# Float64 weights decoded with one VectorE step fewer, without low parts by DMA, and with rows negated on GpSimd

## The chip, the cores and the metric

One core of one Trainium2 chip runs the whole kernel. The number that counts is the device time of an execution in microseconds, the median of three runs. The engines named below are TensorE (PE in the rows), VectorE (DVE), ScalarE (ACT), GpSimd (POOL) and SyncE (SP), which only starts DMAs here.

## The reference

Causal attention over 2 batches, 12 heads, 448 positions and head size 64 gives 896 tokens of width 768. Two feed-forward layers with 2048 hidden units follow, with two different gates:

```python
x = attn_out.transpose(0, 2, 1, 3).reshape(896, 768)
h = x @ w_in;   g = h * cos(h);                                x = g @ w_out
h = x @ w_in2;  g = h if h >= 1 else 0 if h <= -1 else (h + 1)**2 / 4
return (g @ w_out2).astype(float32)
```

Queries, keys and values are float32. The weights are float64 (a product of float32 numbers with a numpy scalar), and the answer has to be close to that of float64 arithmetic.

## The kernel before

**Arithmetic.** TensorE multiplies in a rounded float32 format. So each operand is split in a high part `hi` (a copy in that format) and a low part `lo` (the value minus `hi`), and each product is three matmuls: hi*hi, hi*lo, lo*hi.

**Decoding.** A float64 weight lies in SBUF as two 32-bit words, `low` and `high`. From them a float32 is put together: sign and exponent from `high`, 20 bits of mantissa from `high`, 3 from `low`. ScalarE takes `Abs` of `high` read as float32 (line 236, rows of `w_out` 726). VectorE clamps that to the range of exponents (240, 584), masks and shifts it left by 3 (242, 585), ORs in the top 3 bits of `low` (247, 590) and then the sign and the top exponent bit of `high` (250, 593).

**Input stage of a layer.** `w_in` comes in 16 units of 768 x 128 numbers (units 0 to 15 for the first layer, 16 to 31 for the second). `load_unit` brings one into one of two `raw` buffers, the decoded unit lies in one of two `f` buffers, and ScalarE copies `whi` (258). For `wlo` there are three ways. Units 0 and 1 use GpSimd (267). Units 3 to 15 (`UNIT_LO_BY_DMA`) use ScalarE for -f (262) and then a DMA that adds `f` to it (264). The others use VectorE (267). TensorE multiplies the units two by two (line 632); a pair is 72 matmuls. A gate follows for each unit: ScalarE and VectorE in turn, lines 686 to 705.

**Output stage of a layer.** `w_out` comes in 16 blocks of rows (n = 0 to 15, even blocks first; the last six use the `raw` buffers too). They are decoded into `ws` and one of two halves is negated by ScalarE (`rows_minus`, 573). The output product is done in Strassen's way with seven products over four slices, 28 steps t = 0 to 27. Each step needs four splits, `shi`, `slo` from `ws` and `s`, `s` from the gates `gs` (lines 758 to 768), and is 18 matmuls (line 800). Sums of two `ws` or two `gs` parts are accumulating DMAs from GpSimd's queue (576).

**What sets the order.** Attention runs in an order given by tables (`PLACES`, `SHIFTS`, `DECODE`, `FILL`); units 0, 1 and 2 are begun there. Behind it everything is planned by the class `Plan`: each operation has an engine, a cost in us and a list of operations that it needs; a delay (`LAG`) stands for the way from one engine to the next, above all for DMAs. `Plan` works back from TensorE's order to the latest start of each operation, and then issues on each engine, of what is ready, the most urgent. The result is a fixed order for each engine: an engine that waits for one instruction does nothing behind it. In the plan's names A, K, M, H, O are the steps of a unit (abs, first and second half of the decoding, `whi`, `wlo`), a, k, m, g those of a row block.

Of the kernel before, what the change touches and what calls it, by code (L numbers as in the profile page):

```python
# [15 lines left out]
U32 = mybir.dt.uint32  # L16
AF = mybir.ActivationFunctionType
# [15 lines left out]
EXP_MIN = _float_of(897 << 20)  # L33
EXP_MAX = _float_of((1150 << 20) | 0xFFFFF)
# [46 lines left out]
UNIT_LO_BY_DMA = set(range(3, 16))  # L81
# [3 lines left out]
class Plan:  # L85


    LAG = {"PE": 0.1, "ACT": 0.15, "DVE": 0.1, "SP": 4.6, "POOL": 5.0}
# [8 lines left out]
    def add(self, name, engine, us, make, after=(), at=-9.0):  # L97
        after = [a for a in after if a in self.ops]
        op = dict(engine=engine, us=us, make=make, after=[(a, self.LAG[self.ops[a]["engine"]]) for a in after], at=at)
        if engine == "PE":  # L100
            if self.last_pe:
                op["after"].append((self.last_pe, 0.0))
            self.last_pe = name
        assert name not in self.ops
        self.ops[name] = op

    def run(self):
# [17 lines left out]
        while any(waiting.values()):  # L125
            best = None
            for e, names in waiting.items():
                can = []
                for n in names:
                    if all("end" in ops[a] for a, _ in ops[n]["after"]):  # L130
                        r = max([ops[a]["end"] + lag for a, lag in ops[n]["after"]] + [ops[n]["at"]])
# [12 lines left out]
            self.log.append((start, e, n, ops[n]["late"]))  # L144
            ops[n]["make"]()
# [17 lines left out]
def attention_then_two_ffn(  # L163
# [60 lines left out]

    def decode_unit(u):
# [4 lines left out]
        words = raw.bitcast(U32).rearrange("p (m two) -> p m two", two=2)  # L230
        low, high = words[:, :m, 0], words[:, :m, 1]
        full = f_p.tile([P, UW], F32, tag="f", name=f"f{u}")
        fl = full[:, :m]
        bits = full.bitcast(U32)[:, :m]

        nc.scalar.activation(  # L236
            out=fl, in_=raw.bitcast(F32).rearrange("p (m two) -> p m two", two=2)[:, :m, 1], func=AF.Abs
        )
# [3 lines left out]
        nc.vector.tensor_scalar(  # L242
            out=bits, in0=bits, scalar1=0x07FFFFFF, scalar2=3,
            op0=ALU.bitwise_and, op1=ALU.logical_shift_left,
        )
        yield
        nc.vector.scalar_tensor_tensor(  # L247
            out=bits, in0=low, scalar=29, in1=bits, op0=ALU.logical_shift_right, op1=ALU.bitwise_or,
        )
        nc.vector.scalar_tensor_tensor(  # L250
            out=bits, in0=high, scalar=0xC0000000, in1=bits, op0=ALU.bitwise_and, op1=ALU.bitwise_or,
        )
# [328 lines left out]
    def decode_bits(bits, low, high, part):  # L581
        if part == 0:
            fl = bits.bitcast(F32)
            nc.vector.tensor_scalar(out=fl, in0=fl, scalar1=EXP_MAX, scalar2=EXP_MIN, op0=ALU.min, op1=ALU.max)
            nc.vector.tensor_scalar(
                out=bits, in0=bits, scalar1=0x07FFFFFF, scalar2=3,
                op0=ALU.bitwise_and, op1=ALU.logical_shift_left,
            )
        else:
            nc.vector.scalar_tensor_tensor(  # L590
                out=bits, in0=low, scalar=29, in1=bits, op0=ALU.logical_shift_right, op1=ALU.bitwise_or,
            )
            nc.vector.scalar_tensor_tensor(  # L593
                out=bits, in0=high, scalar=0xC0000000, in1=bits, op0=ALU.bitwise_and, op1=ALU.bitwise_or,
            )

# [11 lines left out]
    def ffn(k):  # L608
# [8 lines left out]
        def add(name, engine, us, make, after=(), at=-9.0):  # L617
            plan.add(f"{k}{name}", engine, us, make, [a[1:] if a[0] == "@" else f"{k}{a}" for a in after], at)
# [100 lines left out]
        def rows_parts(n):  # L719
            j, i, q = spot(ORDER[n])  # L720
            words = raw_rows[n].bitcast(U32).rearrange("p (h m two) -> p h m two", two=2, h=2)
            return ws[j].bitcast(U32)[:, q : q + 2, i], words[:, :, :, 0], words[:, :, :, 1]

        def rows_abs(n):
            bits, _, high = rows_parts(n)
            nc.scalar.activation(out=bits.bitcast(F32), in_=high.bitcast(F32), func=AF.Abs)  # L726

        def rows_bits(n, which):
            decode_bits(*rows_parts(n), which)

        def rows_minus(n):
            j, i, q = spot(ORDER[n])
            minus(ws[j][:, q + 1, i])
# [156 lines left out]
        for f in range(0, KF, 2):  # L890
# [14 lines left out]
            for i in (f, f + 1):  # L905
# [7 lines left out]
                else:  # L913
                    add(f"G{i}", "ACT", 2.85, partial(start_gate, i), need)
# [12 lines left out]
        for n in range(KF):  # L927
# [27 lines left out]
        def add_split(t):  # L955
# [130 lines left out]
```

## Time and profile before

| | us |
|---|---|
| three runs | 547.92, 547.98, 548.77 |
| median | 547.98 |
| the profiled execution | 548.55 |
| its span in the trace | 546.8 |
| mean granted TensorE clock | 0.987 |

The span runs from the first to the last instruction in the trace; 1.75 us of the profiled execution lie around it. In time order the stages are: attention to about 84 us, the first layer's input products to 211, its output products to 325, the second layer's input products to 441, its output products to the end.

### The profile page before, as it was taken

What the parts mean: (1) busy time and instruction counts of PE and PEld (TensorE: products, weight loads), DVE (VectorE), ACT (ScalarE), POOL (GpSimd) and SP (SyncE); (2) the same over time, 40 slices, a digit from 0 to 9 for tenths busy, and PEclk for the clock granted to TensorE, in tenths of its full rate; (3) what the DMA queues carried; (4) which work ended last, traced back from release to release, by engine and by line L of the source; (5) the groups of instructions that cost most, each with busy time, mean ns of one, the idle gap of its engine ahead of it and who ended that gap; (6) DMA issues with size and microseconds to landing.
All of it is one profiled execution on the core that took longest, in us unless ns stands there. A gap on an engine that the chain in (4) does not pass through costs nothing.

```text
span 546.8 us, 7835 instructions
## 1 busy us (share of the span) xinstructions
PE 523.4 (96%) x2865; PEld 454.6 (83%) x2865; DVE 449.4 (82%) x637; ACT 374.1 (68%) x618; POOL 106.4 (19%) x159
## 2 busy tenths in 40 slices
PE   8999999989999799994999999999999999999997
PEld 3676668778988789993899999898898999999996
DVE  6878788798898788981999889899999878996661
ACT  5999875786887587861656554978797897645430
POOL 2667672012122011241000000000101014300000
PEclk9999999989999899998899999999999999999999
DMA  8731136989999584799203047396768459950111
GB/s 302 254 120 41 39 109 226 244 216 229 277 261 282 136 208 121 155 225 238 50 2 115 1 125 261 128 236 179 237 202 236 120 154 205 205 116 17 52 50 51
DMA packets 45574, 87.80 MB, mean 161 GB/s; under 512 B 2784, under 2 KB 32096, under 8 KB 45536
## 3 DMA queue, kind: packets, MB, share of 16 engines
q1 hardware_dynamic: 36464, 61.40, 33.6%
q0 software_dynamic: 8784, 25.56, 25.8%
q8 instruction: 22, 0.36, 0.3%
q10 hardware_dynamic: 288, 0.34, 0.2%
q14 instruction: 16, 0.13, 0.1%
HBM read 58.98 MB, written 2.75 MB: 113 GB/s over the span
## 4 chain that ended last, share of the span: by engine, by line
PE 75%; DMA 11%; DVE 5%; issue 4%; ACT 4%; POOL 1%; DVEq 0%; POOLq 0%; ACTq 0%
PE m L800 35%; PE m L632 28%; DMA wlo<-f 7%; DMA raw<-in_moe_w_in 3%; PE o L437 3%; PE tx L412 2%; PE sa L323 2%; ACT p L373 1%; PE sb L323 1%; PE tw L412 1%; ACT f L236 1%; PE tz L412 1%; PE warm L516 1%; PE sc L308 1%; DVE f L250 1%
## 5 line engine op out<-in xcount | busy, mean ns | idle before, releaser
L632 PE MATMUL m<-x,whi 128*128 128x512 f32 (+2 forms) x728 | 207.3, 366 | 0.0
L800 PE MATMUL m<-s,shi 128*128 128x448 f32 x648 | 186.4, 369 | 7.4 <-ACT shi L758 7.4
L632 PEld LDWEIGHTS m<-x,whi 128*128 128x128 f32 x728 | 136.2, 190 | 14.4
L632 PE MATMUL m<-x,wlo 128*128 128x512 f32 (+2 forms) x364 | 133.7, 367 | 7.9 <-DMA wlo<-f 7.9
L800 PEld LDWEIGHTS m<-s,shi 128*128 128x128 f32 x648 | 122.5, 189 | 18.8 <-ACT shi L758 7.8
L800 PE MATMUL m<-s,slo 128*128 128x448 f32 x324 | 119.5, 369 | 0.0
L632 PEld LDWEIGHTS m<-x,wlo 128*128 128x128 f32 x364 | 69.4, 191 | 16.3 <-DMA wlo<-f 9.2
L800 PEld LDWEIGHTS m<-s,slo 128*128 128x128 f32 x324 | 61.2, 189 | 5.9 <-DVE slo L766 0.5
L766 DVE TENSOR_TENSOR slo<-ws,shi 128x768 fp32r<-128x768 f32 x56 | 53.0, 951 | 11.6 <-ACT shi L758 11.6
L576 POOL DMA_DIRECT2D ws<-ws x24 | 21.7, 903 | 189.2 <-ACT ws L573 136.7
L236 ACT ACTIVATE f<-raw 128x768 f32<-128x768 f32 x32 | 29.1, 912 | 31.7 <-DMA raw<-in_moe_w_in 17.4
L758 ACT CAST shi<-ws 128x768 fp32r<-128x768 f32 x56 | 46.0, 825 | 2.7 <-PE m L800 2.7
L758 ACT CAST s<-gs 128x896 fp32r<-128x896 f32 x24 | 22.6, 942 | 30.6 <-PE m L800 30.6
L760 ACT ACTIVATE s<-gs 128x896 fp32r<-128x896 f32 x30 | 28.5, 950 | 19.3 <-PE m L800 12.9
L576 POOL DMA_DIRECT2D gs<-gs x24 | 22.3, 930 | 89.3 <-DVE s L768 30.5
L768 DVE SCALAR_TENSOR_TENSOR s<-gs,s 128x896 fp32r<-128x896 f32 x30 | 32.6, 1085 | 5.7 <-ACT s L760 5.7
L258 ACT CAST whi<-f 128x768 fp32r<-128x768 f32 x32 | 26.5, 828 | 12.8 <-DVE f L250 11.5
L766 DVE TENSOR_TENSOR s<-gs,s 128x896 fp32r<-128x896 f32 x24 | 26.1, 1087 | 9.5 <-ACT s L758 9.5
L726 ACT ACTIVATE ws<-rows 128x768 f32<-128x768 f32 x32 | 28.9, 909 | 6.8 <-DMA rows<-in_moe_w_out 6.8
L250 DVE SCALAR_TENSOR_TENSOR f<-raw,f 128x768 uint32<-128x768 uint32 x32 | 31.1, 971 | 1.1
L593 DVE SCALAR_TENSOR_TENSOR ws<-rows,ws 128x768 uint32<-128x768 uint32 x32 | 30.7, 958 | 1.1
L247 DVE SCALAR_TENSOR_TENSOR f<-raw,f 128x768 uint32<-128x768 uint32 x32 | 30.7, 960 | 0.0
(103 smaller groups left out, 770.6 us busy)
## 6 DMA issues: line engine op xcount, KB each, us to landing
raw<-in_moe_w_in SPq DMA_DIRECT2D x32, 768.0 KB, 6.0
rows<-in_moe_w_out SPq DMA_DIRECT2D x32, 768.0 KB, 5.3
gs<-gs POOLq DMA_DIRECT2D x24, 448.0 KB, 7.0
ws<-ws POOLq DMA_DIRECT2D x24, 384.0 KB, 7.6
wlo<-f POOLq DMA_DIRECT2D x13, 384.0 KB, 6.2
v<-in_v SPq DMA_DIRECT2D x12, 256.0 KB, 2.8
k<-in_k SPq DMA_DIRECT2D x12, 224.0 KB, 3.8
qr<-in_q SPq DMA_DIRECT2D x11, 224.0 KB, 4.2
```

The lines of the kernel that those rows point to most:

```text
L236: nc.scalar.activation(out=fl, in_=raw.bitcast(F32).rearrange("p (m two) -> p m two", two=2)[:, :m, 1], func=AF.Abs)
L247: nc.vector.scalar_tensor_tensor(out=bits, in0=low, scalar=29, in1=bits, op0=ALU.logical_shift_right, op1=ALU.bitwise_or,)
L250: nc.vector.scalar_tensor_tensor(out=bits, in0=high, scalar=0xC0000000, in1=bits, op0=ALU.bitwise_and, op1=ALU.bitwise_or,)
L576: nc.gpsimd.dma_start(out=to, in_=what, accum_op=ALU.add)
L593: nc.vector.scalar_tensor_tensor(out=bits, in0=high, scalar=0xC0000000, in1=bits, op0=ALU.bitwise_and, op1=ALU.bitwise_or,)
L632: nc.tensor.matmul(o, w[a][:, c, :], x_of(t, c)[:, s], start=(c == first and n == 0), stop=(c == last and n == 2),)
L726: nc.scalar.activation(out=bits.bitcast(F32), in_=high.bitcast(F32), func=AF.Abs)
L758: nc.scalar.copy(out=hi, in_=src)
L760: nc.scalar.mul(out=hi, in_=src, mul=-1.0)
L766: nc.vector.tensor_tensor(out=lo, in0=src, in1=f32(hi), op=ALU.subtract)
L768: nc.vector.scalar_tensor_tensor(out=lo, in0=src, scalar=-1.0, in1=f32(hi), op0=ALU.mult, op1=ALU.subtract)
L800: nc.tensor.matmul(o, l[:, i, d * P : (d + 1) * P], r[:, i], start=(p in (0, 2, 4) and j == 0 and i == 0 and n == 0), stop=(j == NJ - 1 an ...
```

## The change

The bits are made in another way. `Abs` on ScalarE now has a scale of 2^16, so that the top exponent bit ends up where the later shift by 3 drops nothing that is needed, and the clamp's bounds are scaled with it; the mask step is not needed any more. The 3 bits of `low` come from its top byte: ScalarE reads the byte (step 8 in memory), computes byte / 32 - 31 / 64 and writes it as an integer into the word `low` (step 2 words). VectorE then does two steps behind the clamp: `low` = (`high` AND sign) OR `low`, in place in the raw buffer, and then bits = (bits << 3) OR `low`. Units 0, 1 and 2 (`early`) keep four VectorE steps and have no byte step; there the shift stands in the second half, with the other two.

No unit takes its low part by DMA any more: units 3 to 15 use VectorE. The negation of rows goes from ScalarE to GpSimd. The plan's costs follow, and its delays behind DMAs are 6.0 us (SP) and 7.0 us (POOL) instead of 4.6 and 5.0, so the order changes everywhere behind the attention.

```diff
+UP = 2.0**16
+EXP_MIN = _float_of(897 << 20) * UP
+EXP_MAX = _float_of((1150 << 20) | 0xFFFFF) * UP
...
-UNIT_LO_BY_DMA = set(range(3, 16))
+UNIT_LO_BY_DMA = set()
...
-    LAG = {"PE": 0.1, "ACT": 0.15, "DVE": 0.1, "SP": 4.6, "POOL": 5.0}
+    LAG = {"PE": 0.1, "ACT": 0.15, "DVE": 0.1, "SP": 6.0, "POOL": 7.0}
...
+    def decode_words(fl, raw, early=False):
+
+        low, high, byte = words_of(raw, fl)
+        nc.scalar.activation(out=fl, in_=high.bitcast(F32), func=AF.Abs, scale=UP)
+        if not early:
+            nc.scalar.activation(out=low, in_=byte, func=AF.Copy, scale=1.0 / 32, bias=-31.0 / 64)
+
+    def decode_clamp(fl):
+        nc.vector.tensor_scalar(out=fl, in0=fl, scalar1=EXP_MAX, scalar2=EXP_MIN, op0=ALU.min, op1=ALU.max)
+
+    def decode_bits(fl, raw, early=False):
+        bits = fl.bitcast(U32)
+        low, high, _ = words_of(raw, fl)
+        if early:
...
+            return
+        nc.vector.scalar_tensor_tensor(
+            out=low, in0=high, scalar=0x80000000, in1=low, op0=ALU.bitwise_and, op1=ALU.bitwise_or,
+        )
+        nc.vector.scalar_tensor_tensor(
+            out=bits, in0=bits, scalar=3, in1=low, op0=ALU.logical_shift_left, op1=ALU.bitwise_or,
+        )
...
+        early = u <= RAW_BUFS
+        decode_words(fl, raw, early)
         yield
-        nc.vector.tensor_scalar(out=fl, in0=fl, scalar1=EXP_MAX, scalar2=EXP_MIN, op0=ALU.min, op1=ALU.max)
-
-        nc.vector.tensor_scalar(
-            out=bits, in0=bits, scalar1=0x07FFFFFF, scalar2=3,
-            op0=ALU.bitwise_and, op1=ALU.logical_shift_left,
-        )
+        decode_clamp(fl)
         yield
...
         def rows_minus(n):
             j, i, q = spot(ORDER[n])
-            minus(ws[j][:, q + 1, i])
+            t = ws[j][:, q + 1, i]
+            nc.gpsimd.tensor_scalar(out=t, in0=t, scalar1=-1.0, scalar2=1.0, op0=ALU.mult, op1=ALU.mult)
...
-                add(f"A{f}", "ACT", 0.87, partial(decode, u), [f"L{f}"] + ([f"O{f - 2}"] if f > 1 else before(f"O{KF - 2 + f}")))
-            add(f"K{f}", "DVE", 1.1, partial(decode, u), [f"A{f}"])
+                add(f"A{f}", "ACT", 1.8, partial(decode, u), [f"L{f}"] + ([f"O{f - 2}"] if f > 1 else before(f"O{KF - 2 + f}")))
+            add(f"K{f}", "DVE", 0.56, partial(decode, u), [f"A{f}"])
...
-            add(f"g{n}", "ACT", 0.47, partial(rows_minus, n), [f"m{n}"])
+            add(f"g{n}", "POOL", 0.65, partial(rows_minus, n), [f"m{n}"], lag=0.15)
```

Three places of the new order. In names such as `shi011` the first digit is the layer (0 or 1), the rest the step t; `raw16` and `f16` are unit 16, `rows014` is row block 14 of the first layer; the number behind the underscore only tells buffers apart.

VectorE at the start of the first layer's input stage, unit 3, before:

```order
L240 TENSOR_SCALAR f3_1384<-f3_1384 128x768
L242 TENSOR_SCALAR f3_1384<-f3_1384 128x768
L267 TENSOR_TENSOR wlo2_1391<-f2_1325,whi2_1390 128x768
L247 SCALAR_TENSOR_TENSOR f3_1384<-raw3_1245,f3_1384 128x768
L250 SCALAR_TENSOR_TENSOR f3_1384<-raw3_1245,f3_1384 128x768
```

The same place in the change:

```order
L246 TENSOR_SCALAR f3_1383<-f3_1383 128x768
L262 SCALAR_TENSOR_TENSOR raw3_1245<-raw3_1245 128x768
L265 SCALAR_TENSOR_TENSOR f3_1383<-f3_1383,raw3_1245 128x768
L296 TENSOR_TENSOR wlo2_1391<-f2_1325,whi2_1390 128x768
L246 TENSOR_SCALAR ws0_1376<-ws0_1376 128x2x384
L262 SCALAR_TENSOR_TENSOR rows00_1380<-rows00_1380 128x768
L265 SCALAR_TENSOR_TENSOR ws0_1376<-ws0_1376,rows00_1380 128x2x384
L296 TENSOR_TENSOR wlo3_1403<-f3_1383,whi3_1402 128x768
```

A unit has three steps instead of four, and its `wlo` follows on VectorE, behind a row block.

ScalarE among the first layer's output products, at the first load for the second layer, before:

```order
L760 ACTIVATE s012_2600<-gs001_1460 128x896
L573 ACTIVATE ws3_1379<-ws3_1379 128x384
L236 ACTIVATE f16_2612<-raw16_2561 128x768
L758 CAST shi011_2616<-ws3_1379 128x768
L758 CAST shi012_2627<-ws0_1376 128x768
L760 ACTIVATE s013_2637<-gs011_1716 128x896
L758 CAST shi013_2646<-ws1_1377 128x768
```

The same place in the change:

```order
L775 ACTIVATE s012_2590<-gs001_1461 128x896
L773 CAST shi011_2606<-ws3_1379 128x768
L775 ACTIVATE s013_2617<-gs011_1708 128x896
L773 CAST shi012_2623<-ws0_1376 128x768
L241 ACTIVATE f16_2633<-raw16_2567 128x768
L243 ACTIVATE raw16_2567<-raw16_2567 128x768
L773 CAST shi013_2650<-ws1_1377 128x768
```

The abs of unit 16, which needs the load, moves from ahead of `shi011` to behind `shi012`, and the byte step stands behind it.

VectorE some 15 us earlier, at the decoding of row block 14, whose raw buffer unit 16 gets next, before:

```order
L766 TENSOR_TENSOR s08_2494<-gs001_1460,s08_2494 128x896
L766 TENSOR_TENSOR s09_2515<-gs011_1716,s09_2515 128x896
L766 TENSOR_TENSOR slo09_2506<-ws1_1377,shi09_2505 128x768
L590 SCALAR_TENSOR_TENSOR ws3_1379<-rows014_2381,ws3_1379 128x2x384
L593 SCALAR_TENSOR_TENSOR ws3_1379<-rows014_2381,ws3_1379 128x2x384
```

The same place in the change:

```order
L781 TENSOR_TENSOR s09_2494<-gs011_1708,s09_2494 128x896
L781 TENSOR_TENSOR slo09_2505<-ws1_1377,shi09_2504 128x768
L246 TENSOR_SCALAR ws3_1379<-ws3_1379 128x2x384
L781 TENSOR_TENSOR s010_2522<-gs021_1956,s010_2522 128x896
L262 SCALAR_TENSOR_TENSOR rows014_2427<-rows014_2427 128x768
L265 SCALAR_TENSOR_TENSOR ws3_1379<-ws3_1379,rows014_2427 128x2x384
```

The low part of step 10's gates (`s010`) now stands ahead of the two steps that set the raw buffer free.

## Rows read from the trace of the kernel before

**Rows 1.** First part of the page: busy us, share, instructions.

```profile
PE 523.4 (96%) x2865; PEld 454.6 (83%) x2865; DVE 449.4 (82%) x637; ACT 374.1 (68%) x618; POOL 106.4 (19%) x159
```

**Rows 2.** Waits of PE over the span: total us, times, longest.

```profile
PE m L632 <- DMA wlo<-f: 7.9, 3, 4.1
PE m L800 <- ACT shi L758: 7.4, 1, 7.4
```

**Rows 3.** Timeline of PE: start, us, what, idle before and releaser.

```profile
103.91 0.50 PE L632 MATMUL m<-x,wlo 128*128 128x512 f32 x1 [1.12 <-DMA wlo<-f]
120.21 0.69 PE L632 MATMUL m<-x,wlo 128*128 128x384 f32 x1 [2.64 <-DMA wlo<-f]
180.80 0.44 PE L632 MATMUL m<-x,wlo 128*128 128x384 f32 x1 [4.11 <-DMA wlo<-f]
259.48 0.74 PE L800 MATMUL m<-s,shi 128*128 128x448 f32 x1 [7.39 <-ACT shi L758]
```

**Rows 4.** Busy us by stage: PE, PEld, DVE, ACT, POOL, PEclk, DMA.

```profile
84.00:211.00 127.00, 119.12 (x575) 106.85 (x574) 109.89 (x140) 93.50 (x130) 19.52 (x22) 0.97 0.84 226
260.00:325.00 65.00, 65.00 (x309) 58.60 (x308) 59.83 (x76) 37.58 (x51) 0.84 (x1) 0.98 0.20 58
325.00:441.00 116.00, 116.00 (x578) 104.66 (x577) 105.60 (x139) 90.65 (x115) 6.79 (x8) 1.00 0.68 198
```

**Rows 5.** The same view in stretches of ten us.

```profile
70.00:80.00 10.00, 9.48 (x82) 7.03 (x80) 9.74 (x18) 6.48 (x18) 6.92 (x10) 1.00 0.29 86
120.00:130.00 10.00, 9.79 (x41) 8.81 (x42) 8.59 (x11) 6.96 (x10) 2.95 (x3) 0.84 0.80 208
180.00:190.00 10.00, 9.20 (x41) 8.91 (x42) 8.13 (x11) 6.73 (x10) 0.85 (x1) 0.83 0.38 108
260.00:270.00 10.00, 10.00 (x42) 8.65 (x41) 10.00 (x13) 6.94 (x10) 0.84 (x1) 0.84 0.27 58
```

**Rows 6.** Chain that ended last: start, us, what.

```profile
211.18 26.05 PE m L800 x126
...
238.93 18.87 DMA raw<-in_moe_w_in
```

**Rows 7.** Groups by line and shape in 84-211: count, busy us, mean ns.

```profile
L236 ACT ACTIVATE f<-raw 128x768 f32<-128x768 f32 x14 | 12.6, 909 | 12.2 <-DMA wlo<-f 12.2
L262 ACT ACTIVATE wlo<-f 128x768 fp32r<-128x768 f32 x13 | 10.9, 840 | 0.0
L573 ACT ACTIVATE ws<-ws 128x384 f32<-128x384 f32 x11 | 5.5, 510 | 0.0
...
L250 DVE SCALAR_TENSOR_TENSOR f<-raw,f 128x768 uint32<-128x768 uint32 x14 | 13.4, 958 | 0.5
L242 DVE TENSOR_SCALAR f<-f 128x768 uint32<-128x768 uint32 x14 | 7.8, 560 | 0.5
```

**Rows 8.** The same view over the span, VectorE's `wlo`.

```profile
L267 DVE TENSOR_TENSOR wlo<-f,whi 128x768 fp32r<-128x768 f32 x17 | 16.1, 949 | 0.5 <-ACT whi L258 0.5
```

**Rows 9.** Timeline of VectorE, a decoding step beside GpSimd work.

```profile
77.23 1.22 DVE L250 SCALAR_TENSOR_TENSOR f<-raw,f 128x768 uint32<-128x768 uint32 x1
```

**Rows 10.** Waits of ScalarE before the gates, over the span.

```profile
ACT ax L699 <- PE m L632: 9.6, 6, 2.7
ACT ax L686 <- PE m L632: 8.2, 5, 2.8
```

**Rows 11.** Groups by shape over the span: GpSimd on 128x384.

```profile
L392 POOL TENSOR_SCALAR p<-p,ra 128x384 f32<-128x384 f32 x22 | 13.3, 617 | 16.4 <-DVE ra L380 12.2 <-ACT p L373 1.5 <-PE tx L412 1.0
```

**Rows 12.** Timeline of GpSimd: three steps alone, and beside VectorE's decoding.

```profile
60.55 1.54 POOL L392 TENSOR_SCALAR p<-p,rb 128x448 f32<-128x448 f32 x3
...
71.87 2.94 POOL L392 TENSOR_SCALAR p<-p,rb 128x448 f32<-128x448 f32 x3 [1.12 <-DVE rb L380]
```

**Rows 13.** Timeline of ScalarE: the cast for product 10.

```profile
237.30 0.95 ACT L758 CAST s<-gs 128x896 fp32r<-128x896 f32 x1 [1.88 <-PE m L800]
```

**Rows 14.** DMA issues of 235-262: count, KB each, median us to landing.

```profile
raw<-in_moe_w_in SPq DMA_DIRECT2D x2, 768.0 KB, 18.4
```

More of the change, by code (lines that the diff above doesn't have):

```diff
@@ L95, in __init__, with add @@
         self.last_pe = None
[L97 to L99 removed]
+    def add(self, name, engine, us, make, after=(), lag=None):
+        after = [(a, self.ops[a]["lag"]) for a in after if a in self.ops]
+        op = dict(engine=engine, us=us, make=make, after=after, lag=self.LAG[engine] if lag is None else lag)
         if engine == "PE":
@@ L130, in run @@
                     if all("end" in ops[a] for a, _ in ops[n]["after"]):
-                        r = max([ops[a]["end"] + lag for a, lag in ops[n]["after"]] + [ops[n]["at"]])
+                        r = max([ops[a]["end"] + lag for a, lag in ops[n]["after"]] + [-9.0])
                         can.append((r, n))
@@ L223, in load_unit, with words_of @@
         raws[u] = raw
+    def words_of(raw, like):
+        n = like.shape[1] if len(like.shape) == 2 else like.shape[1] * like.shape[2]
+        words = raw.bitcast(U32).rearrange("p (m e) -> p m e", e=2)
+        parts = words[:, :n, 0], words[:, :n, 1], raw.bitcast(U8).rearrange("p (m e) -> p m e", e=8)[:, :n, 3]
+        if len(like.shape) == 3:
+            parts = [t.rearrange("p (h m) -> p h m", h=like.shape[1]) for t in parts]
+        return parts
+    def decode_words(fl, raw, early=False):
[9 more added lines that the diff above has]
+        if early:
+            nc.vector.tensor_scalar(
+                out=bits, in0=bits, scalar1=3, scalar2=0, op0=ALU.logical_shift_left, op1=ALU.bitwise_or
+            )
+            nc.vector.scalar_tensor_tensor(
+                out=bits, in0=low, scalar=29, in1=bits, op0=ALU.logical_shift_right, op1=ALU.bitwise_or,
+            )
+            nc.vector.scalar_tensor_tensor(
+                out=bits, in0=high, scalar=0x80000000, in1=bits, op0=ALU.bitwise_and, op1=ALU.bitwise_or,
+            )
+            return
+        nc.vector.scalar_tensor_tensor(
+            out=low, in0=high, scalar=0x80000000, in1=low, op0=ALU.bitwise_and, op1=ALU.bitwise_or,
+        )
+        nc.vector.scalar_tensor_tensor(
+            out=bits, in0=bits, scalar=3, in1=low, op0=ALU.logical_shift_left, op1=ALU.bitwise_or,
+        )
     def decode_unit(u):
@@ L229, in decode_unit @@
         m = n * width
-        words = raw.bitcast(U32).rearrange("p (m two) -> p m two", two=2)
-        low, high = words[:, :m, 0], words[:, :m, 1]
         full = f_p.tile([P, UW], F32, tag="f", name=f"f{u}")
         fl = full[:, :m]
-        bits = full.bitcast(U32)[:, :m]
-        nc.scalar.activation(
-            out=fl, in_=raw.bitcast(F32).rearrange("p (m two) -> p m two", two=2)[:, :m, 1], func=AF.Abs
-        )
+        early = u <= RAW_BUFS
+        decode_words(fl, raw, early)
         yield
-        nc.vector.tensor_scalar(out=fl, in0=fl, scalar1=EXP_MAX, scalar2=EXP_MIN, op0=ALU.min, op1=ALU.max)
-        nc.vector.tensor_scalar(
-            out=bits, in0=bits, scalar1=0x07FFFFFF, scalar2=3,
-            op0=ALU.bitwise_and, op1=ALU.logical_shift_left,
-        )
-        yield
[L247 to L252, printed above, removed]
+        decode_clamp(fl)
+        yield
+        decode_bits(fl, raw, early)
         if u < RAW_BUFS:
@@ L579, in subtract @@
         nc.vector.tensor_tensor(out=to, in0=a, in1=b, op=ALU.subtract)
[L581 to L595, printed above, removed]
     def three(t, n):
@@ L615, in ffn, with add @@
         x = x1 if k == 0 else None
-        def add(name, engine, us, make, after=(), at=-9.0):
-            plan.add(f"{k}{name}", engine, us, make, [a[1:] if a[0] == "@" else f"{k}{a}" for a in after], at)
+        def add(name, engine, us, make, after=(), lag=None):
+            plan.add(f"{k}{name}", engine, us, make, [a[1:] if a[0] == "@" else f"{k}{a}" for a in after], lag)
         def before(name):
@@ L720, in rows_parts, with rows_words, rows_clamp, rows_bits @@
             j, i, q = spot(ORDER[n])
[L721 to L729, printed above, removed]
+            return ws[j][:, q : q + 2, i], raw_rows[n]
+        def rows_words(n):
+            decode_words(*rows_parts(n))
+        def rows_clamp(n):
+            decode_clamp(rows_parts(n)[0])
+        def rows_bits(n):
+            decode_bits(*rows_parts(n))
         def rows_minus(n):
             j, i, q = spot(ORDER[n])
-            minus(ws[j][:, q + 1, i])
+            t = ws[j][:, q + 1, i]
+            nc.gpsimd.tensor_scalar(out=t, in0=t, scalar1=-1.0, scalar2=1.0, op0=ALU.mult, op1=ALU.mult)
         pieces = {}
```

19 lines of the change are left out of this document (9 added, 10 removed).

## The prediction, made before the result was known

> **What bounds the kernel now.** The page's first part comes first: TensorE's matmuls are busy 96% of the span [rows 1], so what can be won is mostly TensorE's idle time and its slow time. Next the waits by TensorE [rows 2]: behind the attention there are two kinds. It waits 7.9 us in three places for the DMA that adds `f` into `wlo`, and 7.4 us once for ScalarE's `shi`. The timeline places them [rows 3]: 1.12, 2.64 and 4.11 us in the first FFN's input products, 7.39 us at 259.48 among its output products. From 260 on it is busy without a gap (65.00 of 65 us, then 116.00 of 116 [rows 4]), so the second FFN has only something to lose.
>
> Each long wait costs twice. In ten-microsecond stretches [rows 5] the granted clock is 0.84 at 120-130, 0.83 at 180-190 and 0.84 at 260-270, right behind the idle times; a lower mean is time at 1.2 instead of 2.4 GHz. That loses 1.6, 1.7 and 1.6 us beside the waits.
>
> The chain of waits says what stands behind the long one [rows 6]: a `w_in` load (raw of unit 16, the second FFN's first) issued at 238.93 and under way for 18.87 us. ScalarE's abs of this unit stands in its queue ahead of shi011, the split of product 11, so TensorE waits for a load that none of its products there needs.
>
> **Part by part.** First the thirteen low parts by DMA (units 3 to 15). Before, one is a ScalarE pass of 0.840 us [rows 7] and an accumulating DMA, which ends in TensorE's waits. Now a VectorE subtraction of 0.949 us [rows 8] does it. The three waits go, and two slow stretches: 7.9 + 3.3 = 11.2 us. What is late next is VectorE. In 84-211 it is busy 109.89 us [rows 4]. Thirteen subtractions at 0.949 less thirteen mask-and-shift steps at 0.560 [rows 7] are +5.1; twelve rows of `w_out` lose that step too, -6.7: 108.3 us. Without waits and slow clock the stretch lasts 127 - 11.2 = 115.8, so VectorE is 93% full. In 325-441 it is 91% full (105.60 of 116) and TensorE waits for nothing [rows 4], so 93% with a much shorter chain per unit (no DMA between ScalarE and TensorE) should hold, nearly. I leave 1.5 us for it.
>
> Second, the new prices. ScalarE gets a byte pass for 29 units and 32 rows. No row shows reading bytes at a step of 8 or writing words at a step of 2. The lower end is a plain pass with constants, 0.840; reading at a step costs at most 0.909 (which `Abs` takes) [rows 7]; the upper end, if the strided write halves the rate, is an estimate of 2 x 0.909 = 1.82. I take 0.84, the nearest row in kind. VectorE's two steps of the form (a op s) op b are 0.958 with one strided input [rows 7]; the new first one has both inputs and the output strided. I take 0.958; the upper end is 1.22, the slowest such row [rows 9].
> The Trainium skill (SBUF — State Buffer, Door 1: The DMA port swizzle, the box on "cachelines") says that two accesses to a 16-byte line are enough for full rate; a step of 8 bytes gives two. 0.958 strided against 0.949 not [rows 7, 8] agrees for reads; for writes no run here shows it yet. By it both prices stay at their lower ends and the sum is unchanged.
>
> ScalarE's room: in 84-211 it is busy 93.50 [rows 4]. Thirteen passes for `wlo` go and thirteen byte passes come, 0; by the new order eleven rows instead of thirteen are decoded before product 0, -1.8; their byte passes +9.2; eleven negations at 0.510 move to GpSimd, -5.6: 95.3 of 115.8. In 325-441: 90.65 + 12 x 0.84 for units, -0.9 (one row fewer), +9.2, -6.2 (twelve negations): 102.8 of 116, and up to 9.6 of the rest are waits for TensorE's results before a gate [rows 10], which nothing fills. That is tight but fits: 0.3 us. VectorE loses 0.56 for each unit and row there and has room.
>
> Third, 32 negations on GpSimd, 0.617 us each [rows 11], hidden: only the last pair stands ahead of a split that TensorE is close to, shi011, and by the order that is some 5 us early (an estimate). Beside GpSimd work VectorE's steps stretched to 1.22 from 0.958, while three GpSimd steps that take 1.54 took 2.94 [rows 9, 12]: GpSimd gives way more than VectorE. Eleven negations at some 0.3 us are 3 us for VectorE in 84-211, 96% then; that is inside the 1.5 above.
>
> Fourth, the boundary. The new order puts the abs of unit 16 behind shi012, two products later. A product takes 26.05 / 7 = 3.72 us (seven products of 18 matmuls) [rows 6], so shi013 is due not at 251.9 but at 259.4. Abs, byte pass and shi013 take 0.91 + 0.84 + 0.82, so the load must have landed by 256.8. It is issued when row 14 is decoded: 238.9 now [rows 6]. The new order has the low part of product 10 ahead of that; it waits for ScalarE's cast at 237.30, held back by TensorE [rows 13], so 238.2 + 1.09 + 0.95 + 0.96 = 241.2. The two loads there took 18.4 us in the median [rows 14], beside accumulating DMAs from GpSimd's queue. Those stay; the load starts later but behind a backlog that has run on meanwhile, so I take a landing at 258.0, where it was 257.8: a wait of 1.2. Bounds: nothing, or 18.87 again, landing at 260.1, a wait of 3.3 and a slow stretch of 1.6.
>
> Fifth, the attention: for units 0 and 1 the shift moves down to just before the two long steps at 72-78, where VectorE is busy 9.74 of 10 us and TensorE already idles 0.5 [rows 5]. Between 0 and 2 x 0.80; I take 0.5. Unit 2 keeps its count.
>
> **Sum**, on the profiled execution (548.55; span 546.8 and 1.75 around it): -11.2 - 7.4 - 1.6 + 1.5 + 1.2 + 0.5 + 0.3 = -16.7, so 531.85. The median of the runs is 0.57 below the profiled one: 531.3.
>
> **Rivals.** A: the boundary is not cured. For it speaks that the load leaves 2.3 us later and the DMA engines stay full there. With the load at 18.87 us it is 531.3 - 1.2 + 4.9 = 535; with the full 9.0 us lost, 539. Against it: two products of slack.
> B: VectorE becomes the bound of the first FFN. By the rows the stretch is 3 us in 84-211; if each of the eleven negations stops VectorE for its whole 0.617 (+6.8) VectorE has 115.1 of 115.8, and order does the rest: about +4, 535.5. With the first step at 1.22 too, 25 of them add 6.6, 542. The Trainium skill (SBUF — State Buffer, SBUF: two separate sides) states such a lock: a VectorE step with two SBUF inputs and a GpSimd step that reads SBUF exclude each other for a whole instruction. The rows agree only in part: VectorE lost 0.26 at most, GpSimd paid 1.4.
> C, on the other side: the byte pass is dear. It binds ScalarE in both input stretches: room 115.8 - 95.3 - 8.2 = 12.3 and 116 - 102.8 - 9.6 = 3.6 [rows 4, 10], with 24 and 23 byte passes. Extra e each gives 47e - 15.9; it eats the 16.7 from e = 0.69, that is from 1.53 us on. At 1.82 it is +30, 561. Only the strided write and the byte input speak for it.
> D: it does nothing, since new waits fill the gaps exactly; nothing points to it but chance.
>
> **How the numbers follow.** Forecast 0.62, A 0.14, B 0.14, C 0.07, D 0.03. What a measurement of this kernel can tell is about 0.2%, 1.1 us. All of forecast, A and B is faster, 0.90; D is the same, 0.03; C is slower, 0.07. If all waits go at no cost it is 548.0 - 20.2 = 527.8, so the range begins at 527.5; it ends at 541, which takes in A and most of B and leaves out C and D.
>
> **What would show it.** TensorE's waits: none for a DMA of `wlo`, no granted clock under 0.95 between 110 and 200; the first output product begins about 11 us earlier, near 200. The byte pass at 0.84 to 0.91 us, the first new VectorE step near 0.96. ScalarE's wait for raw of unit 16 is left, but short for TensorE: under 3 us. In the second FFN still no wait. Wrong would be: waits by TensorE for VectorE's low parts in the first FFN (B), for `whi` or gates in the second (C), or again some 7 us at the boundary (A).

## The result and the profile after

The median is 533.07 us (four runs, 532.24 to 533.47) against 547.95 (four runs, 545.88 to 548.77): a ratio of 0.9732, 95% interval 0.9703 to 0.9761. The forecast was 531.3, in a range of 527.5 to 541.0. The profiled execution took 532.24 us, with a span of 530.4 and a mean granted clock of 0.997.

The first table to make from two such traces is the start of each stage: it says where the 16.4 us between the spans lie before any wait is looked at.

| stage | before, us | after, us | difference |
|---|---|---|---|
| attention, to the first input product | 83.4 | 83.5 | +0.1 |
| first layer, input products | 127.6 | 115.7 | -11.9 |
| first layer, output products | 113.5 | 108.7 | -4.8 |
| second layer, input products | 115.9 | 115.6 | -0.3 |
| second layer, output products | 106.3 | 106.8 | +0.5 |

The first part of the page answers [rows 1]:

```profile
PE 517.1 (97%) x2865; PEld 451.3 (85%) x2865; DVE 432.8 (82%) x589; ACT 396.5 (75%) x634; POOL 120.3 (23%) x178
```

TensorE's longest waits (total us, times, longest) answer [rows 2]:

```profile
PE m L815 <- ACT shi L773: 3.3, 1, 3.3
PE sb L352 <- ACT p L402: 1.5, 2, 1.4
```

The wait for `wlo<-f` is gone from the list, and of the 7.4 us for `shi` 3.3 are left. TensorE's timeline places them ([rows 3]):

```profile
250.86 1.11 PE L815 MATMUL m<-s,shi 128*128 128x448 f32 x2 [3.31 <-ACT shi L773]
```

And the chain of waits shows the first output product and the load of unit 16 (start, us, what; [rows 6]):

```profile
199.38 12.41 PE m L815 x60
...
229.71 18.70 DMA raw<-in_moe_w_in
```

The busy times by stage and in stretches of ten us (PE, PEld, DVE, ACT, POOL, PEclk, DMA; [rows 4, 5]):

```profile
83.00:199.00 116.00, 116.00 (x585) 104.86 (x582) 107.10 (x127) 97.46 (x130) 18.50 (x21) 1.00 0.68 202
308.00:424.00 116.00, 116.00 (x579) 104.93 (x578) 92.13 (x112) 103.10 (x127) 14.45 (x20) 1.00 0.67 190
...
70.00:80.00 10.00, 8.53 (x70) 5.78 (x69) 9.79 (x18) 5.32 (x15) 6.08 (x7) 1.00 0.27 82
180.00:190.00 10.00, 10.00 (x45) 8.26 (x44) 9.46 (x11) 8.31 (x12) 1.32 (x2) 1.00 0.48 126
240.00:250.00 10.00, 7.55 (x38) 6.66 (x36) 1.92 (x3) 1.56 (x3) 0.85 (x1) 1.00 1.07 254
250.00:260.00 10.00, 9.14 (x37) 8.01 (x38) 8.59 (x11) 8.74 (x12) 0.00 (x0) 0.83 0.12 24
```

Both input stages hold TensorE busy throughout at full clock, with VectorE at 107.1 and ScalarE at 97.5 of 116 us in the first, ScalarE at 103.1 in the second. At 240-250 VectorE and ScalarE do almost nothing while the DMA engines are full: both stand behind one load. The slow stretch behind the wait (0.83) is the only one left.

The prices that no row of before had, by line and shape (count, busy us, mean ns; [rows 7 to 9, 11]):

```profile
L243 ACT ACTIVATE rows<-rows 128x768 uint32<-128x768 uint8 x32 | 29.1, 909 | 0.0
L262 DVE SCALAR_TENSOR_TENSOR rows<-rows 128x768 uint32<-128x768 uint32 x32 | 30.5, 953 | 0.3 <-ACT rows L243 0.2
L262 DVE SCALAR_TENSOR_TENSOR raw<-raw 128x768 uint32<-128x768 uint32 x29 | 28.6, 985 | 0.3 <-ACT raw L243 0.2
L748 POOL TENSOR_SCALAR ws<-ws 128x384 f32<-128x384 f32 x32 | 25.9, 811 | 236.6 <-DVE ws L265 121.7 <-issue 79.8 <-ACT ws L241 19.2
```

The nearest row of before to the first new VectorE step is the first OR of a row block, whose output is not strided:

```profile
L590 DVE SCALAR_TENSOR_TENSOR ws<-rows,ws 128x768 uint32<-128x768 uint32 x32 | 30.4, 951 | 0.1
```

### The profile page after: what moved, and what is told of

It is laid out like the page before. It is cut to its first block, busy times and chain, and to the rows that moved or that the text cites. A ratio compares the mean times of both kernels' runs of the same rounds, so it can differ in the third digit from the quotient of the medians.

```text
span 530.4 us, 7822 instructions
## 1 busy us (share of the span) xinstructions
PE 517.1 (97%) x2865; PEld 451.3 (85%) x2865; DVE 432.8 (82%) x589; ACT 396.5 (75%) x634; POOL 120.3 (23%) x178
## 4 chain that ended last, share of the span: by engine, by line
PE 85%; DVE 7%; DMA 4%; ACT 3%; issue 1%; DVEq 0%; ACTq 0%
PE m L645 41%; PE m L815 30%; PE o L466 4%; DMA raw<-in_moe_w_in 4%; PE m L517 2%; PE sa L352 2%; PE tx L441 2%; PE sb L352 1%; DVE s L781 1%; DVE slo L781 1%; PE sc L337 1%; PE tw L441 1%; PE warm L545 1%; PE tz L441 1%; DVE nma L380 1%
## 5 line engine op out<-in xcount | busy, mean ns | idle before, releaser
L645 PE MATMUL m<-x,whi 128*128 128x512 f32 (+2 forms) x728 | 204.8, 362 | 0.0
L645 PEld LDWEIGHTS m<-x,whi 128*128 128x128 f32 x728 | 134.4, 188 | 14.2
L645 PE MATMUL m<-x,wlo 128*128 128x512 f32 (+2 forms) x364 | 131.9, 362 | 0.0
L748 POOL TENSOR_SCALAR ws<-ws 128x384 f32<-128x384 f32 x32 | 25.9, 811 | 236.6 <-DVE ws L265 121.7
L645 PEld LDWEIGHTS m<-x,wlo 128*128 128x128 f32 x364 | 68.3, 188 | 7.0
L716 DVE TENSOR_TENSOR gs<-m,ax 128x896 f32<-128x896 f32 x16 | 17.5, 1091 | 22.6 <-ACT ax L714 18.8
L265 DVE SCALAR_TENSOR_TENSOR ws<-ws,rows 128x768 uint32<-128x768 uint32 x32 | 30.9, 964 | 1.1
L296 DVE TENSOR_TENSOR wlo<-f,whi 128x768 fp32r<-128x768 f32 x30 | 28.8, 960 | 3.4 <-ACT whi L287 3.4
L262 DVE SCALAR_TENSOR_TENSOR rows<-rows 128x768 uint32<-128x768 uint32 x32 | 30.5, 953 | 0.3 <-ACT rows L243 0.2
```

The source lines that it names most:

```text
L262: nc.vector.scalar_tensor_tensor(out=low, in0=high, scalar=0x80000000, in1=low, op0=ALU.bitwise_and, op1=ALU.bitwise_or,)
L265: nc.vector.scalar_tensor_tensor(out=bits, in0=bits, scalar=3, in1=low, op0=ALU.logical_shift_left, op1=ALU.bitwise_or,)
L296: e.tensor_tensor(out=lo[:, :m], in0=fl, in1=f32(hi)[:, :m], op=ALU.subtract)
L645: nc.tensor.matmul(o, w[a][:, c, :], x_of(t, c)[:, s], start=(c == first and n == 0), stop=(c == last and n == 2),)
L748: nc.gpsimd.tensor_scalar(out=t, in0=t, scalar1=-1.0, scalar2=1.0, op0=ALU.mult, op1=ALU.mult)
```

## The experiments

The runs of each group share a chip and the runs of the kernel before, whose medians were 548.13, 548.64 and 548.18 us. Ratios are to these. Stage lengths are from the profiled executions.

### Group 1: the boundary, and the parts one by one

**The load counted at 15 us in the changed kernel** (called "late abs" from here on).

```diff
-add(f"L{f}", "SP", 0.1, partial(load_unit, base + f), [...])
+add(f"L{f}", "SP", 0.1, partial(load_unit, base + f), [...], lag=15.0)
```

> The changed kernel with one number added: the plan counts 15 us instead of 6 for the two first loads of the second layer, so ScalarE's abs of unit 16 stands two splits later, behind shi015, and that of unit 17 later too; nothing else moves but the neighbours. Theory (the last wait is the place of the abs in ScalarE's queue, while the load itself takes 18.7 us): the 3.3 us wait of TensorE near 251 and the 0.83 clock in 250-260 go, 3.3 + 1.6 = 4.9 us, so 528 (527.0 to 529.5), with the load's 18 us unchanged. Rival (the wait is the DMA engines' backlog, and splits behind it need a summed part just as late): a wait of 2 to 3.3 us comes back at one of the next splits or low parts, 531 to 533.

528.24 us, ratio 0.9663 [0.9633, 0.9692]. The abs of unit 16 now stands three `shi` later than in the changed kernel. The first output stage takes 104.6 us instead of 108.7, with no wait by TensorE above 0.5 us behind the attention. The DMA issues of 225-262 (count, KB each, median us to landing), of the changed kernel and then of this one:

```profile
raw<-in_moe_w_in SPq DMA_DIRECT2D x2, 768.0 KB, 17.9
```

```profile
raw<-in_moe_w_in SPq DMA_DIRECT2D x2, 768.0 KB, 17.8
```

The load is as slow as before; it only has nobody behind it any more. So the residual wait was the place of the abs. It is worth some 4 us: 4.1 in that stage, 4.8 between the two medians. This version beats both kernels.

**Low parts by DMA again, all else as changed.**

```diff
-UNIT_LO_BY_DMA = set()
+UNIT_LO_BY_DMA = set(range(3, 16))
```

> The changed kernel with the low parts of units 3 to 15 by accumulating DMA again (the plan orders anew). Theory (the DMA chain of the low parts was the cost in the first layer's input products): TensorE waits again for wlo<-f, 4 to 9 us with slow clock behind it, first output product 6 to 12 us later than at 199.4, total 539 to 545. ScalarE gets 13 x 0.84 = 10.9 us more in 83 to 199 (97.5 + 10.9 = 108.4 of 116), which can add to it. Rival (the freed VectorE step and the new order are the gain, the DMA was only where the wait showed): less than 1.5 us later, 533 to 534.5.

549.32 us, ratio 1.0038 [1.0007, 1.0070]: dearer than either theory had it, and not even as good as before. The first input stage takes 135.0 us (the profiled execution, 545.83, is the fastest of the twelve), and the output stage behind it 102.9, without a wait at the boundary. TensorE's waits first, then the busy times of the ten us around the longest, then the DMA that ended it, from the chain of waits (start, us):

```profile
PE m L645 <- DMA wlo<-f: 14.7, 5, 7.9
```

```profile
130.00:140.00 10.00, 4.17 (x11) 3.36 (x12) 6.88 (x8) 6.67 (x11) 2.24 (x3) 0.66 1.06 304
```

```profile
125.05 10.73 DMA wlo<-f
```

ScalarE now has the byte pass and the negated copy for each unit, GpSimd's queue has the negations besides these DMAs, and the DMA of the longest wait takes 10.73 us in full DMA engines (share 1.06). This run does not tell these three apart. What it shows is that the rest of the change, the freed VectorE step with it, brings nothing while the low parts go by DMA.

**The kernel before, low parts by VectorE.**

```diff
-UNIT_LO_BY_DMA = set(range(3, 16))
+UNIT_LO_BY_DMA = set()
```

> The kernel before with one edit: low parts of units 3 to 15 by VectorE, four VectorE steps of decoding kept. Theory (the freed step is what makes room for the low parts): VectorE has 109.9 + 13 x 0.949 = 122.2 us of work in a stretch that lasts 115.8 without waits, so it becomes the bound: the stretch ends at 122 to 128 instead of 127, TensorE waits for VectorE steps (wlo, f); total 543 to 551. Rival (the DMA alone was the cost, the step fewer is not needed): waits gone, 11.2 us gained, 536 to 538.

545.37 us, ratio 0.9971 [0.9948, 0.9995]: 0.3% faster, inside the theory's range, but not by its way. The first input stage shrank to 117.2 us, 1.5 above what the changed kernel takes; the output stage grew from 113.5 to 121.7. The busy times of a stretch that holds the first stage (to 201) and the next nine us, and TensorE's longest wait:

```profile
84.00:210.00 126.00, 124.34 (x615) 111.68 (x616) 119.98 (x150) 90.76 (x123) 9.42 (x11) 1.00 0.64 183
```

```profile
PE m L800 <- ACT shi L758: 13.1, 1, 13.1
```

VectorE is busy 120.0 of these 126 us, and TensorE waits 13.1 us in one place behind them. Whether that wait is again the abs, or VectorE's backlog, is asked in group 2.

**The kernel before, with the longer delays in its plan.**

```diff
-    LAG = {..., "SP": 4.6, "POOL": 5.0}
+    LAG = {..., "SP": 6.0, "POOL": 7.0}
```

> The kernel before with the changed kernel's delays in the plan alone (6.0 and 7.0 us behind DMAs instead of 4.6 and 5.0). Theory (the order alone buys little, since the low parts' DMAs take 6 to 10 us and ScalarE and VectorE hold the work before them): waits for wlo<-f of 5 to 10 us remain, the boundary keeps 3 to 7 us; total 544 to 549. Rival (the longer delays are what removes the waits, decoding has little to do with it): 532 to 538.

546.60 us, ratio 0.9979 [0.9949, 1.0008]: no difference that can be told. TensorE's waits only moved:

```profile
PE m L632 <- DMA wlo<-f: 10.1, 4, 3.8
PE m L800 <- DVE c L823: 4.3, 1, 4.3
```

### Group 2: the late abs without the rest, and prices

**The kernel before, late abs only.**

```diff
-after=[(a, self.LAG[self.ops[a]["engine"]]) for a in after]
+after=[(a, 15.0 if a in ("1L0", "1L1") else self.LAG[self.ops[a]["engine"]]) for a in after]
```

> The kernel before with one edit: its plan counts 15 us for the two first loads of the second layer, so ScalarE's abs of unit 16 stands behind shi014 and not ahead of shi011. Low parts by DMA, decoding in four VectorE steps as before. Theory (the boundary wait is the place of the abs, nothing else): its 7.4 us and the slow stretch of 1.6 go, the wlo waits stay: 548.0 - 9.0 = 539 (537.5 to 541). Rival (the splits there need late summed parts anyway, from full DMA engines): most of the wait comes back at another split, 543 to 547.

539.88 us, ratio 0.9855 [0.9810, 0.9901], within 0.9 us of the theory. The first output stage takes 104.6 us; `wlo<-f` still costs 7.1 us in three waits.

**The kernel before, late abs and low parts by VectorE** (the two edits above together).

> The kernel before with two edits: low parts of units 3 to 15 by VectorE, and 15 us counted for the two first loads of the second layer (abs of unit 16 behind shi015). Four VectorE steps of decoding, no byte pass, negations on ScalarE. With the low parts alone the first input stage ended at 202.2 (before 211.2) and the wait at the boundary grew to 13.1 us. Theory (the freed VectorE step is worth only what VectorE lacked in that stage, 118.2 - 115.8 = 2.4 us, and the boundary is a matter of the abs): 545.4 - 13.1 - 1.6 = 530.7 (529 to 533), within 2 to 4 us of the changed kernel with the late abs (528.2). Rival (VectorE's backlog of the fourth step is what made the boundary late, and shows again as another wait there): 535 to 542.

541.71 us, ratio 0.9896 [0.9852, 0.9940]: the theory fails, the rival holds. The first input stage is as short as in the run without the late abs (117.3 us), the output stage takes 115.0. TensorE waits 8.3 us for `shi` though the abs is out of the way. ScalarE's timeline shows for what, and the busy times show VectorE ahead of it; the last line is from GpSimd's timeline:

```profile
244.54 0.95 ACT L760 ACTIVATE s<-gs 128x896 fp32r<-128x896 f32 x1 [4.74 <-DMA gs<-gs]
249.55 0.95 ACT L760 ACTIVATE s<-gs 128x896 fp32r<-128x896 f32 x1 [4.06 <-DMA gs<-gs]
250.82 3.02 ACT L758 CAST shi<-ws 128x768 fp32r<-128x768 f32 x4
```

```profile
220.00:230.00 10.00, 9.38 (x47) 8.37 (x46) 9.90 (x14) 5.58 (x8) 1.70 (x2) 1.00 1.04 229
```

```profile
230.14 0.84 POOL L576 DMA_DIRECT2D gs<-gs  x1 [5.84 <-DVE s L766]
```

The splits wait for sums that accumulating DMAs make, and four `shi` stand behind. These DMAs follow VectorE's splits and gates: GpSimd's queue stands 5.84 us for one such split, and VectorE is busy 9.9 of 10 us throughout 210-240. The last of these DMAs then takes 12.3 us itself. I had priced the fourth step by what VectorE lacked within the input stage (2.4 us); here its backlog is paid in the next stage.

**Late abs, negations on ScalarE again.**

```diff
-            nc.gpsimd.tensor_scalar(out=t, in0=t, scalar1=-1.0, scalar2=1.0, op0=ALU.mult, op1=ALU.mult)
+            minus(t)
...
-            add(f"g{n}", "POOL", 0.65, partial(rows_minus, n), [f"m{n}"], lag=0.15)
+            add(f"g{n}", "ACT", 0.47, partial(rows_minus, n), [f"m{n}"])
```

> The changed kernel with the late abs (528.2), and the negations of rows on ScalarE again. Theory (they are hidden on either engine): 527.5 to 529.2; ScalarE in 83 to 199 at about 97.5 + 5.6 = 103 of 116, VectorE's steps there shorter by at most 2 us in sum. Rival B (GpSimd stops VectorE): 1 to 3 us faster than 528.2. Rival (ScalarE was the next bound): 1.5 to 4 us slower.

530.39 us, ratio 0.9689 [0.9647, 0.9731] beside 0.9663 [0.9633, 0.9692] with the negations on GpSimd: a little slower, but the intervals overlap and the two did not run on one chip. The first lines of the two pages, with the negations on GpSimd and then here:

```profile
PE 517.5 (98%) x2865; PEld 450.4 (85%) x2865; DVE 432.8 (82%) x589; ACT 396.6 (75%) x634; POOL 119.9 (23%) x178
```

```profile
PE 517.8 (98%) x2865; PEld 451.7 (85%) x2865; DVE 427.8 (81%) x589; ACT 408.5 (77%) x666; POOL 94.3 (18%) x146
```

For the same 589 steps VectorE is busy 5.0 us longer with the 32 negations on GpSimd, 0.16 us for each, and the kernel is not slower for it. The second output stage takes 110.4 us instead of 106.8; its chain has one slow accumulating DMA (`gs<-gs`, from 450.92 on, 11.60 us), and TensorE waits behind it, with a slow stretch (granted clock 0.83 at 460-470). TensorE's timeline:

```profile
464.35 0.68 PE L815 MATMUL m<-s,shi 128*128 128x448 f32 x2 [0.95 <-ACT shi L773]
465.62 0.47 PE L815 MATMUL m<-s,slo 128*128 128x448 f32 x1 [0.60 <-DVE slo L781]
```

Rival B's price is out: GpSimd does hold VectorE up, but without its steps nothing got faster. Whether the 2 us are the place of the negations stays open.

**Late abs, the abs done twice.**

```diff
         nc.scalar.activation(out=fl, in_=high.bitcast(F32), func=AF.Abs, scale=UP)
         if not early:
+            nc.scalar.activation(out=fl, in_=high.bitcast(F32), func=AF.Abs, scale=UP)
+        if not early:
             nc.scalar.activation(out=low, in_=byte, func=AF.Copy, scale=1.0 / 32, bias=-31.0 / 64)
```

> The changed kernel with the late abs (528.2), and the abs of the 29 units and 32 rows done twice (0.91 us more each on ScalarE, same result, same order): a byte pass as dear as 1.82 us. Theory (the room worked out for rival C: 12.3 and 3.6 us in the two input stages, 24 and 23 passes): 24 x 0.91 - (115.8 - 97.5 - 8.2 = 10.1) = 11.7, and 23 x 0.91 - (115.7 - 103.1 - 8.1 = 4.5) = 16.4: 528.2 + 28 = 556 (550 to 562). Rival (waits for gates shrink when ScalarE is late, so more of it is hidden): 536 to 548.

552.04 us, ratio 1.0081 [1.0045, 1.0117], 23.8 us above the late abs alone: inside the theory's range. But the stages are not as worked out. The first input stage takes 124.2 us (+8.5; forecast +11.7), the second 115.9 (+0; forecast +16.4) and the second output stage 118.8 instead of 106.8. In 314-430 ScalarE is busy 112.21 of 116 us and TensorE loses nothing; the loss is in the next stage, where TensorE waits 7.6 us in one place for ScalarE's split (`s`, the line 775 of the change):

```profile
314.00:430.00 116.00, 116.00 (x578) 104.59 (x576) 87.44 (x104) 112.21 (x135) 10.73 (x16) 1.00 0.56 171
430.00:548.00 118.00, 105.58 (x504) 95.78 (x502) 82.20 (x94) 72.85 (x95) 21.52 (x24) 0.95 0.52 116
```

So a byte pass of 1.8 us would have made the change slower than no change, even with the late abs. The end of rival C was priced rightly to some 4 us; the place where it is paid was wrong.

### Group 3: the freed step itself, and what is left

**Late abs, VectorE's clamp done twice.**

```diff
-    def decode_clamp(fl):
+    def decode_clamp(fl, early=False):
         nc.vector.tensor_scalar(out=fl, in0=fl, scalar1=EXP_MAX, scalar2=EXP_MIN, op0=ALU.min, op1=ALU.max)
+        if not early:
+            nc.vector.tensor_scalar(out=fl, in0=fl, scalar1=EXP_MAX, scalar2=EXP_MIN, op0=ALU.min, op1=ALU.max)
...
-        decode_clamp(fl)
+        decode_clamp(fl, early)
```

> The changed kernel with the late abs (528.2), and VectorE's clamp done twice for the 29 units and 32 rows with three steps (0.56 us more each, same result, same order): VectorE's freed step is spent again, all other parts of the change stay. Theory (the freed step is what carries the low parts on VectorE): VectorE has 107.4 + 25 x 0.56 = 121.4 us of work in the first input stage of 115.9, runs late, and the late sums of the output stage make TensorE wait: 535 to 543. Rival (the late abs, the negations on GpSimd and the order carry it): 528 to 531.5.

538.84 us, ratio 0.9830 [0.9795, 0.9864]: 10.6 us dearer than the late abs alone, in the theory's range and far from the rival's. The profiled executions differ by 8.7 us: 1.0 by the end of the attention, 5.9 in the first input stage (121.6 us) and 2.1 in the output stage behind it (106.7), so most of it is paid in the stage of the added steps, unlike in the run with four steps in group 2. The busy times of the first stage show TensorE idle for 3.5 us beside a VectorE at 97%:

```profile
84.00:200.00 116.00, 112.54 (x552) 100.26 (x549) 112.94 (x142) 94.52 (x126) 17.08 (x19) 0.99 0.63 190
```

**Late abs, the old delays elsewhere.**

```diff
-    LAG = {..., "SP": 6.0, "POOL": 7.0}
+    LAG = {..., "SP": 4.6, "POOL": 5.0}
```

> The changed kernel with the late abs (528.2), and the plan's other delays behind DMAs as before (4.6 and 5.0 us; 15 stays for the two loads). Theory (the delays matter little once no low part goes by DMA): 527.5 to 531. Rival (the order needs the longer delays for the accumulating DMAs of the output stages): 532 to 537.

528.57 us, ratio 0.9640 [0.9609, 0.9670]: no difference to the late abs alone (0.9663) that can be told.

**Late abs, the shift of units 0 to 2 back in the first half.**

```diff
-    def decode_clamp(fl):
+    def decode_clamp(fl, early=False):
         nc.vector.tensor_scalar(out=fl, in0=fl, scalar1=EXP_MAX, scalar2=EXP_MIN, op0=ALU.min, op1=ALU.max)
+        if early:
+            bits = fl.bitcast(U32)
+            nc.vector.tensor_scalar(
+                out=bits, in0=bits, scalar1=3, scalar2=0, op0=ALU.logical_shift_left, op1=ALU.bitwise_or
+            )
...
         if early:
-            nc.vector.tensor_scalar(
-                out=bits, in0=bits, scalar1=3, scalar2=0, op0=ALU.logical_shift_left, op1=ALU.bitwise_or
-            )
...
```

> The changed kernel with the late abs (528.2), and for units 0 to 2 the shift back in the first half of the decoding, behind the clamp, as the kernel before has it. Theory (the shift in the second half delays TensorE at 70-80 by 0.5 to 1 us: it is busy 8.5 us there, before 9.5): TensorE busy 9.3 to 9.6 us in 70-80, first input product 0.3 to 1 us earlier, total 527.5 to 528.2. Rival (something else delays 70-80, or the work is made up behind): no change there, 528.2 to 529.

527.58 us, ratio 0.9626 [0.9594, 0.9657], against 0.9640 and 0.9630 for its neighbours: the same. TensorE's busy time at 70-80 comes back, yet the first input product starts at 83.4 us, where most kernels with the late shift have it at 83.5 to 84.3, and those of before, with the early shift, at 83.4 to 84.7:

```profile
70.00:80.00 10.00, 9.47 (x80) 7.00 (x80) 9.79 (x18) 6.48 (x18) 6.90 (x10) 1.00 0.31 87
```

The idle time was real, but what of it reaches the end of the attention is too little to tell.

**19 us instead of 15 for the two loads.** The edit is that of the late abs with `lag=19.0`.

> The changed kernel with 19 us counted for the two loads instead of 15: abs of unit 16 one split later still, that of unit 17 some four splits later. Theory (with 15 the load is no longer waited for by TensorE, more is not needed): 527.5 to 529, same as with 15. Rival (the later abs of unit 17 makes the second layer's first units late): 530 to 534, waits for whi or wlo behind 304.

527.88 us, ratio 0.9630 [0.9596, 0.9663]: same as 15. Once the load is off TensorE's path, more room buys nothing.

## Why the prediction was right, step by step

| term | forecast, us | measured, us |
|---|---|---|
| first input stage: waits and slow clock -11.2, VectorE nearly full +1.5 | -9.7 | -11.9 |
| boundary: wait and slow stretch -9.0, late load +1.2 | -7.8 | -4.8 |
| attention | +0.5 | +0.1 |
| ScalarE in the second layer | +0.3 | -0.3 |
| second output stage | no term | +0.5 |
| sum, profiled executions | -16.7 | -16.4 |

That the sums agree within 0.3 us is partly luck: the first input stage came out 2.2 us better than forecast and the boundary 3.0 us worse. What the two terms rest on, the DMAs of the low parts and the place of the abs, was right; both sizes were off.

**First input stage.** The floor worked out for it, 127 less the waits and the slow clock, was 115.8 us, and it took 115.7. The 1.5 us left for a VectorE at 93% were not needed; the other 0.7 us are for the most part that the stage of before lasted 127.6 us, not 127. VectorE was busy 107.1 us there (forecast 108.3), ScalarE 97.5 (forecast 95.3; twelve rows and negations fell in the stage, not eleven). No granted clock is under 1.00 in this stage.

**The boundary is the term that was mis-sized.** Its three steps were these: the abs moves two products back (it did), the load is issued some 30 us behind the first output product (241.2 - 211.2 = 30.0 was forecast, 229.71 - 199.38 = 30.3 came), and it lands sooner than 18.87 us later because the backlog had run on. The last step failed: it took 18.70 us, so the end that the prediction gave as its worse bound came, a wait of 3.3 us (3.31 measured) and a slow stretch. The late abs settles it: a load as slow (17.8 us), no wait, and a stage 4.1 us shorter. The low parts by DMA are not what fills the DMA engines at that place, since they are gone; the accumulating DMAs of the sums are, and they stayed. In 229-249 of the changed kernel their queue (q0) takes most of the 16 engines, the loads' queue (q1) the rest (packets, MB, share):

```profile
q0 software_dynamic: 1092, 3.17, 83.5%
q1 hardware_dynamic: 1409, 1.42, 23.0%
```

The sign named for this place, a wait under 3 us, was missed: it was 3.31. (A small slip in the forecast: by [rows 3] shi011 was due at 259.48 - 7.39 = 252.1 and not at 251.9, which would have made the forecast wait 1.0 us.)

**Prices.** The byte pass takes 0.909 us, the upper end for a strided read and not the 0.84 taken; 25 of them in the first input stage are 1.7 us more for ScalarE, hidden. The first new VectorE step takes 0.953 on rows and 0.985 on units (0.958 taken). By the Trainium skill (SBUF — State Buffer, Door 1: The DMA port swizzle, the box on "cachelines") two accesses to a 16-byte line are enough for full rate, and a step of 8 bytes makes two. For VectorE's writes 0.953 with a strided output against 0.951 without (line 590 before) now agrees. For ScalarE the rows do not bear it out: its two passes that read at a step of 8 bytes take 0.909 and 0.911, where the contiguous pass of before took 0.840 [rows 7]; no run here separates the step from what else differs between these passes.

**The negation** takes GpSimd 0.811 us in the mean, not 0.617, but this mean mixes two cases. Two negations and the VectorE steps beside them, from the timelines of the changed kernel:

```profile
140.13 0.52 POOL L748 TENSOR_SCALAR ws<-ws 128x384 f32<-128x384 f32 x1 [11.13 <-DVE ws L265]
139.96 1.08 DVE L710 TENSOR_TENSOR gs<-m,ax 128x896 f32<-128x896 f32 x1
...
221.67 1.28 POOL L748 TENSOR_SCALAR ws<-ws 128x384 f32<-128x384 f32 x1 [5.61 <-DVE ws L265]
221.49 1.09 DVE L781 TENSOR_TENSOR s<-gs,s 128x896 fp32r<-128x896 f32 x1
222.49 1.27 DVE L781 TENSOR_TENSOR slo<-ws,shi 128x768 fp32r<-128x768 f32 x1
```

Twelve of the 32 start while VectorE is idle or in a step that reads TensorE's result `m`, and take 0.50 to 0.55 us. The other 20 start during a VectorE step between SBUF buffers and take 0.68 to 1.29; 19 of them end 0.37 to 0.38 us after that step has ended, however much of it was left, so GpSimd stands until VectorE is through. The VectorE step that starts beside a negation is in turn up to 0.3 us longer (`slo` 1.27 here, 0.95 elsewhere). The Trainium skill (SBUF — State Buffer, SBUF: two separate sides) states a lock for which the one that starts first keeps the other out for its whole instruction. The trace agrees with it for GpSimd. Its price was small all the same: VectorE lost 0.16 us for each negation in the mean, and the kernel no time. The 0.617 was such a mean too: of its 22 steps in the attention 21 take 0.58 to 0.59 us, and one beside VectorE's decoding 1.28. The forecast's 0.3 us for VectorE was the loss of one meeting, not the mean.

**The medians** differ by 14.9 us and not by the 16.4 of the spans, since the profiled execution after is the fastest of its four (the others 533.05 to 533.47) and that of before, at 548.55, lies above its median. The forecast was carried over with before's offset alone.

**What carries the gain.** The prediction spoke of the low parts, and of the freed step as their cover. The runs show how much that cover is worth. With the low parts by VectorE but four steps: 2.8 us gained, with the late abs 6.9, where the late abs alone gave 8.8. With the step fewer, the byte pass and the negations on GpSimd, but the low parts by DMA: 1.2 us lost. With both: 14.9, and 19.9 with the late abs. Spending the freed step again takes 10.6 of these. The edits are not additive: each needs the room that the other makes.

**Rivals.** A happened in part (3.3 of 7.4 us stayed). B's mechanism is there and too small. C's price did not come; had it come, the end would have been on the slower side: 552.0 us with the late abs, where 561 was forecast without it.

## What to carry to other kernels

Read what an engine lacks in one stage, then ask who starts the next stage with its backlog: the fourth VectorE step looked like 2.4 us in the input stage, and the run with it ended 11.0 us above the forecast made from that (541.7 against 530.7), with the loss in the output stage; and more than half of what ScalarE's doubled abs cost was paid one stage after the one that it filled. Where a wait is for a slow transfer that the waiting engine does not need yet, move the instruction that needs it: counting the load as 15 us instead of 6 in the plan bought some 4 us, while the transfer stayed at 18 us. Test a change of several edits by undoing each alone; here the low parts alone gained 0.3%, and the rest of the change without them nothing.

## What the runs showed of the hardware that was not expected

- ScalarE's pass that reads bytes at a step of 8 and writes 32-bit integers at a step of two words takes 0.909 us for 128x768, the same as `Abs` of a strided float32 (0.911 on rows): byte input and strided write together add nothing to it.
- A 768 KB load takes 4.7 us in the median of the changed kernel (6.0 in the kernel before), and 17.8 to 18.9 at the boundary, where accumulating DMAs from GpSimd's queue run beside it (DMA share 1.07 at 230-250).
- GpSimd's 128x384 step takes 0.50 to 0.55 us alone, and ends 0.37 to 0.38 us behind a VectorE step between SBUF buffers that it started beside (19 of 20), so it took up to 1.29.
